# Inducing-point attention with a PReLU feed-forward layer on one core: the x of batch 1 loaded earlier, in fewer transfers, and its DMA transposes moved forward

## The chip, the cores and the metric

The kernel runs on one core of a Trainium2 chip. The metric is the device time of one execution in microseconds (us). The core has five engines with queues of their own: PE (TensorE, matrix multiply), DVE (VectorE), ACT (ScalarE), POOL (GpSimd) and SP (SyncE, which here does nothing but issue DMAs). DMAs are issued from POOL and from SP and are carried by the core's 16 DMA engines. An engine works through its own instructions in order.

## The reference, cut to what matters

```python
B, N, m, C = (4, 12480, 32, 128)          # x: [B, N, C], inducing: [m, C]
def mab(q, kv):
    s = scale * (q @ kv.transpose(0, 2, 1))
    a = softmax(s)                         # written out with max and sum in the reference
    return a @ kv
h   = mab(I, x)                            # 32 inducing points look at all 12480 tokens of a batch
y   = mab(x, h)                            # every token looks at the 32 rows of h
# the second part, over all B*N = 49920 tokens; w_in [128, 2048], w_out [2048, 128]
t = y @ w_in
g = np.maximum(t, 0.0) + alpha * np.minimum(t, 0.0)
out = g @ w_out
```

So a batch has two passes over its x: the first makes `h` (32 x 128) out of all its tokens, and only then can any of its output be made.

## The kernel before, in words

A batch's 12480 tokens are cut into six blocks of 2048 tokens (u = 0 to 5) and a remainder of 192 (u = 6), taken in `order = [0, 1, 6, 2, 3, 4, 5]`. The output side works on groups g of 512 tokens, four to a block, 25 to a batch.

*First pass.* For batch 0 it is the prologue: x is loaded and turned by PE (`p_xpose`, `p_scores`, `p_pool`). For the batches 1 to 3 it runs beside the output work of the batch before, block by block, in four steps:
- `a_load` (L162): DMAs on POOL bring a block of x into a tile `xn`, cast to bf16, cut into `pieces` DMAs. The pool of `xn` has 6 buffers.
- `a_xpose` (L180): one DMA transpose on SP turns `xn` into `xT`. That pool has 8 buffers (XTS).
- `a_scores` (L310): PE multiplies `xT` by the inducing points, ACT takes exp into `e1`, and SP issues a second DMA transpose, `e1T<-e1` (L321; `e1Tr<-e1r`, L331, for the remainder).
- `a_accum` (L336): PE multiplies `e1T` by `xn` and DVE adds to `hacc`.

When all seven blocks are in, `h_sum`, `h_den`, `h_transpose` and `h_weights` make the batch's `hW`.

*Output side.* `b_scores` (L416) makes the scores of a block against h, writes them to DRAM (`e2d<-e`, L435), `b_rep` (L440) reads them back four times as `rep` (L445), `b_den` and `b_turn` send the denominators the same way (`rt<-rd` L478, `rdT<-rt` L488; all four on SP). For each group 16 chunks are made by `fill`: a PE product `hW` x `rep` into a PSUM bank, which ACT (L542) or DVE (L545) empties as relu into a tile `gt`. PE multiplies `gt` by `W1`, and `finish` (L581) closes the group: DVE turns it (L592), POOL multiplies by the reciprocals (L595) and issues four output DMAs (L608).

*Order of the work.* The order on every engine is written out by hand: `pin` chains each engine's instructions. After the prologue come eight sessions t = 0 to 7, in which groups 0 and 1 of batch 0 are filled by four row strips at once, then a step SESSIONS = 8, then the laned stage, in which the groups pass one after another through four lanes of 32 rows; T0 = 9 is the step at the start of its first group, T0 + m the one at the start of its group m. A table `tasks` gives each step the extra work done there, in the order in which `at` entered it. For batch 1 it is set by the lists `score`, `load` and `cross`: the step at which a block, in the order above, is scored, loaded and turned. A block is accumulated 4 steps after it is scored (the last block 3).

*The prologue's end.* POOL's order there is: x of batch 0, `w_in_b` (L635), `w_out_f` in four DMAs (L640), small constants, then `w_scale` (L682) twice: four products for `W1` (W on the page) and four for `AW` (L686). SP's order is: `winT` (two transposes, L693), `e2d` of block 0, and on. PE uses `W1` from the first session on, `AW` and `winT` at t = 5 (`w_amat`).

Of the kernel before, what the change touches and what calls it, by code (L numbers as in the profile page):

```python
# [19 lines left out]
NQ = 4  # L20
# [16 lines left out]
def kernel(  # L37
# [26 lines left out]


    last = {}

    def pin(bi):
        ins = bi.ins
        e = ins.engine  # L70
        if e in last:
            tc.add_manual_dep(
                ins,
                last[e],
                mybir.DependencyInfo(
                    mybir.DependencyClass.NoSync, mybir.DependencyReason.DATA
                ),
                reason="program order",
            )
        last[e] = ins.name  # L80
        return bi
# [30 lines left out]
    def bank():  # L112
        i = min(idle, key=lambda i: clk.free[i])
        idle.remove(i)
        clk.pe = max(clk.pe, clk.free[i])
        return banks[i]

    def drained(t, engine, ns, pe=0, after=190):
        clk.pe += pe
        start = clk.pe + after  # L120
        if engine == "A":
            clk.act = end = max(clk.act, start) + ns
        else:
            clk.dve = end = max(clk.dve, start) + ns
        i = number[id(t)]
        clk.free[i] = end + 170
        idle.append(i)
# [8 lines left out]
    def new_batch(b):  # L136
        st = Batch()
        st.b = b
        st.xT = {}
        st.xTr = xt_pool.tile([C, JR, PR], bf16, name="xTr", tag="xTr")  # L140
        st.xn = {}
        st.e1T = {}
        st.sc = scale
        st.rs = None
        st.e2 = {}
        st.d = {}
        st.rep = {}
        st.rden = {}
        st.rt = {}
        if b > 0:  # L150
            st.es = work.tile([P, NS + 1], f32, name="es", tag="es")
            st.hacc = work.tile([P, C], f32, name="hacc", tag="hacc")
            nc.vector.memset(st.es[:], 0.0)
            nc.vector.memset(st.hacc[:], 0.0)
        return st
# [6 lines left out]
    def a_load(st, u, pieces=1):  # L162
        t0 = u * SUP
        if u < NS:
            xn = xn_pool.tile([P, NQ, GRP], bf16, name="xn", tag="xn")
            src = x[st.b, t0 : t0 + SUP, :].rearrange("(p q j) c -> p q (j c)", q=NQ, j=NB)
            w = NQ // pieces
            for i in range(pieces):
                pin(nc.gpsimd.dma_start(  # L169
                    out=xn[:, i * w : (i + 1) * w, :], in_=src[:, i * w : (i + 1) * w, :]  # L170
                ))
        else:
            xn = xn_pool.tile([PR, JR, C], bf16, name="xnr", tag="xnr")
            pin(nc.gpsimd.dma_start(
                out=xn[:],
                in_=x[st.b, t0 : t0 + REM, :].rearrange("(p j) c -> p j c", j=JR),
            ))
        st.xn[u] = xn
# [56 lines left out]
    def p_scores(st, u, i):  # L235
        blocks = p_blocks(st, u, i)
        pp, nb = (PR, JR) if u == NS else (P, 2 * NB)
        ps = bank()
        for k, (xt, _) in enumerate(blocks):
            mm(ps[:pp, k * M : (k + 1) * M], xt, IT[:])  # L240
        e1t = head_pool.tile([P, 2 * NB, M], bf16, name="e1t", tag="e1t")
        pin(nc.scalar.activation(  # L242
            out=e1t[:pp, :nb, :].rearrange("p k m -> p (k m)"), in_=ps[:pp, : nb * M],
            func=EXP, scale=scale,
        ))
        drained(ps, "A", 370, 200)
        st.e1T[u, i] = e1t
# [243 lines left out]
    def shape_of(g):  # L491
        return (P, NB, 1) if g < NS * NQ else (PR, JR, 2)

    states = {}
    accs = {}
    left = {}
    begun = set()
# [116 lines left out]
    order = [0, 1, NS] + list(range(2, NS))  # L614
# [16 lines left out]
    pin(nc.sync.dma_start(out=al_f[:], in_=moe_alpha.rearrange("(k p) -> k p", p=P)))  # L631
    for u in order[3:]:
        a_load(st, u, pieces=2)
    w_in_b = const.tile([C, DFF], bf16, name="w_in_b")
    pin(nc.gpsimd.dma_start(out=w_in_b[:], in_=moe_w_in))  # L635
    w_out_f = stage.tile([P, KC, C], f32, name="w_out_f", tag="stage")
# [36 lines left out]
    def alphas():  # L673
        alp = bank()
        pin(nc.tensor.transpose(alp[:, :KC], al_f[:], ident32[:KC, :KC]))
        pin(nc.vector.tensor_copy(out=alT[:], in_=alp[:, :KC]))
        pin(nc.vector.tensor_scalar(
            out=om_al[:], in0=alT[:], scalar1=-1.0, scalar2=1.0, op0=MULT, op1=ADD
        ))
        drained(alp, "D", 300, 60)  # L680

    def w_scale(dst, fac):  # L682
        for j in range(NJ):
            f = fac[:, j::NJ]
            fb = bass.AP(tensor=f.tensor, offset=f.offset, ap=[f.ap[0], f.ap[1], [0, C]])
            pin(nc.gpsimd.tensor_tensor(  # L686
                out=dst[:, j::NJ, :], in0=w_out_f[:, j::NJ, :], in1=fb, op=MULT
            ))
# [27 lines left out]
    n = len(halves)  # L716
    p_xpose(st, *halves[0])
    for i in range(n):
        if i + 1 < n:
            p_xpose(st, *halves[i + 1], last=i + 2 == n)  # L720
        p_scores(st, *halves[i])
        if i == n - 1:
            warm(st)
        if i > 0:
            p_pool(st, *halves[i - 1], first=i == 1)
        if i == 3:
            alphas()
            w_scale(W1, om_al)
            w_scale(AW, alT)
            w_inT()  # L730
# [14 lines left out]
    def tokens(st):  # L745
# [21 lines left out]
        SESSIONS = 8  # L767
        T0 = SESSIONS + 1

        tasks = {}  # L770

        def at(t, fn):
            assert t >= 0, t
            tasks.setdefault(t, []).append(fn)
            if not {"b_rep", "b_turn", "a_load", "a_xpose", "h_sum", "new_batch"} & set(fn.__code__.co_freevars):
                pauses.add(t)
# [9 lines left out]
        for b in range(B):  # L786
            base = T0 + (first[b, 0] if b else -2)
            for s in range(1, NS + 1):
                t = base + 4 * s - AHEAD if b or s > 2 else 4 * s - 2
                nt = t + 4 if s < NS else t + 2  # L790
                at(t, lambda b=b, s=s: b_scores(states[b], s))
                at(t + 1, lambda b=b, s=s: b_rep(states[b], s))
                at(nt, lambda b=b, s=s: b_den(states[b], s))
                at(nt + 1, lambda b=b, s=s: b_turn(states[b], s))
            if b + 1 < B:
                n = b + 1
                E = base + 4 * NS
                if b:
                    lag = (-8, -4, -4, 0, 4, 8, 10) if b > 1 else (-4, 0, 0, 4, 6, 8, 10)
                    score = [base + k for k in lag]  # L800
                    load = [t - 7 for t in score]
                    cross = [t - 5 for t in score]
                    late = 4
                else:
                    score = [T0 + k for k in (2, 4, 4, 6, 8, 10, 11)]
                    load = [0, 0, 5, SESSIONS, T0 + 1, T0 + 3, T0 + 5]
                    cross = [5, 5, 6, T0 + 1, T0 + 3, T0 + 5, T0 + 7]
                    late = 3
                for u, k, c, t in zip(order, score, cross, load):
                    at(k + (late if u == order[-1] else 4), lambda n=n, u=u: a_accum(states[n], u))  # L810
                    at(k, lambda n=n, u=u: a_scores(states[n], u))
                    at(c, lambda n=n, u=u: a_xpose(states[n], u))
                    at(t, lambda n=n, u=u: a_load(states[n], u, pieces=NQ))
                at(score[-1] + 1, lambda n=n: h_sum(states[n]))
                H = score[-1] + late
                at(H, lambda n=n: h_den(states[n]))
                at(H + 1, lambda n=n: h_transpose(states[n]))
                H += 2
                assert H <= E - 6
                at(H, lambda n=n: h_weights(states[n]))  # L820
                at(H, lambda n=n: b_scores(states[n], 0))
                at(H, lambda n=n: h_linear(states[n]))
                at(H + 1, lambda n=n: b_rep(states[n], 0))
                at(E - 4, lambda n=n: b_den(states[n], 0))
                at(E - 3, lambda n=n: b_turn(states[n], 0))
                fn = lambda n=n: states.setdefault(n, new_batch(n))
                tasks.setdefault(load[0], []).insert(0, fn)

        def run_tasks(t):
            for fn in tasks.pop(t, []):  # L830
# [44 lines left out]
        while queue or moving or any(tile):  # L875
            best = []
            taken = {q for _, q, _ in moving}
            for f in range(4):
                if tile[f]:
# [3 lines left out]
                    elif (*y, todo[0]) in seen:  # L883
                        t = max(free_at[f], seen[*y, todo[0]][1] - 100)
                        best.append((t, 1, f, "piece"))
                else:
# [3 lines left out]
                    if f == 0 and queue and sum(map(bool, tile)) + len(moving) < LANES:  # L890
                        ch = (*queue[0], 0)
                        if ch in seen:
                            t = max(free_at[f], seen[ch][1] - 100 - SLOT)
                            best.append((t, 2, f, "start"))
            if fillable():
                since = max(min(clk.free[i] for i in idle) - 40, landed.get(need[0][:2], 0))
                hungry = min(clk.act, clk.dve) < clk.pe + HUNGRY
                for f in range(4):
                    t = max(free_at[f], since)
# [8 lines left out]
            t, _, f, what = min(best, key=lambda x: (max(x[0], clk.pe), x[1]))  # L908
# [27 lines left out]
            else:  # L936
                y, todo = tile[f]
                u = todo.pop(0)
# [67 lines left out]
```

## Time and profile before

| what | value |
|---|---|
| device time, three runs | 573.31, 574.81, 575.17 us; median 574.81 us |
| the profiled execution | 575.11 us; span 573.3 us from first to last instruction |
| mean granted PE clock | 0.980 |
| PE busy | 549.9 us, 96% of the span |
| ACT busy | 509.1 us, 89% |
| DVE busy | 499.5 us, 87% |
| POOL busy | 414.8 us, 72% |
| x loads on POOL (L169) | 72 DMAs of 128 KB, 10 of 256 KB |
| xT DMA transposes on SP | 18; issue 2.0 to 7.3 us, landing 6.2 to 16.1 us after the issue began |
| e1T DMA transposes on SP | 18; issue 1.2 to 2.2 us, landing 3.1 to 9.0 us after the issue began |

Times in the text are us from the start of the span, unless they are durations. In a line of the timeline the first number is the start, the second the duration, "xN" says that N instructions were merged, and brackets tell how long the engine was idle before it. PEclk is the granted clock, 1.00 being full speed. SPq stands for SP's queue of DMA issues. In the traces a batch or a block has no number; which block a DMA carries follows from the order above.

### The profile page before, as it was taken

The page shows a single profiled execution, that of the slowest core. Times are in us where ns is not written, and L with a number is a line of the kernel's source. Part 1 is how long each engine was busy: PE and PEld are TensorE (multiplying, and loading weights), DVE is VectorE, ACT ScalarE, POOL GpSimd, SP SyncE. Part 2 cuts the span into 40 slices and gives each one's busy share as a digit, 9 for nine tenths or more (in the row PEclk, how much of TensorE's full clock was granted, in tenths as well). Part 3 has the DMA queues.
Part 4 walks back from the last instruction along what each step waited for, and adds up shares of the span by engine and source line. Part 5 has one row for each costly group of instructions (what it writes and reads, how often), then busy time and mean ns, then how long its engine had stood idle before and what let it go on. Part 6 is the DMA issues. An engine that isn't in the chain of part 4 may idle for free.

```text
span 573.3 us, 21059 instructions
## 1 busy us (share of the span) xinstructions
PE 549.9 (96%) x8671; PEld 300.6 (52%) x8671; DVE 499.5 (87%) x857; ACT 509.1 (89%) x1014; POOL 414.8 (72%) x612
## 2 busy tenths in 40 slices
PE   4999996999999999999999999999999999999994
PEld 4633552555554545555555555655555555555542
DVE  3687895899989999999998999999988999999971
ACT  2477995999998999999989999999999999999970
POOL 6657584687798499886878976675777677676771
PEclk9995998999999999999999999999999999999998
DMA  9979999996899999987897898544444354444333
GB/s 197 223 140 152 187 139 134 156 166 93 139 168 157 111 166 164 159 140 120 128 177 142 114 163 146 77 91 97 67 88 102 56 100 105 80 75 66 57 56 63
DMA packets 120448, 71.09 MB, mean 124 GB/s; under 512 B 87536, under 2 KB 112480, under 8 KB 120352
## 3 DMA queue, kind: packets, MB, share of 16 engines
q0 software_dynamic: 25008, 38.53, 44.3%
q1 hardware_dynamic: 95200, 30.69, 30.4%
q8 instruction: 68, 1.11, 0.9%
q10 hardware_dynamic: 144, 0.52, 0.2%
q14 instruction: 28, 0.23, 0.2%
HBM read 41.00 MB, written 28.95 MB: 122 GB/s over the span
## 4 chain that ended last, share of the span: by engine, by line
PE 58%; POOL 19%; issue 9%; DMA 6%; ACT 5%; DVE 1%; SPq 1%; POOLq 0%; DVEq 0%; ACTq 0%
PE bank L130 58%; POOL out_dram L608 13%; POOL ob L595 6%; ACT gt L542 5%; DMA xn<-in_x_dram 3%; DMA e1T<-e 2%; DVE gt L545 1%; DMA rdT<-rt 1%; SPq L608 1%; DMA rt<-rd 1%; DMA out_dram<-ob 0%; DVE ot L592 0%; DVE hW L302 0%; PE bank L215 0%; ACT xT L224 0%
## 5 line engine op out<-in xcount | busy, mean ns | idle before, releaser
L130 PE MATMUL bank<-gt,W 32*128 32x512 bf16 (+2 forms) x6016 | 497.4, 377 | 0.6
L542 ACT ACTIVATE gt<-bank 128x512 bf16<-128x512 f32 (+1 forms) x920 | 472.7, 608 | 20.8 <-PE bank L130 17.3
L545 DVE TENSOR_SCALAR gt<-bank 128x512 bf16<-128x512 f32 (+1 forms) x648 | 411.9, 679 | 33.5 <-PE bank L130 28.2
L130 PE MATMUL bank<-rep,hW 32*128 32x512 bf16 (+1 forms) x1600 | 418.5, 374 | 0.8 <-DVE hW L302 0.3
L130 PEld LDWEIGHTS <-W 32*128 32x128 bf16 (+1 forms) x6016 | 232.0, 92 | 171.0 <-issue 89.3
L608 POOL DMA_DIRECT2D out_dram<-ob x384 | 245.9, 667 | 47.9 <-POOL ob L595 28.2
L595 POOL TENSOR_TENSOR ob<-ot,rdT 128x512 f32<-128x512 f32 (+1 forms) x100 | 109.3, 1093 | 92.3 <-DVE ot L592 80.6
L130 PEld LDWEIGHTS <-hW 32*128 32x128 bf16 x1600 | 130.4, 92 | 45.6 <-issue 23.8
L592 DVE STREAM_TRANSPOSE ot<-bank 128x512 f32<-128x512 f32 (+1 forms) x100 | 69.4, 695 | 11.9 <-PE bank L130 11.0
L169 POOL DMA_DIRECT2D xn<-in_x_dram x82 | 46.1, 635 | 4.7 <-DMA xn<-in_x_dram 2.8
L130 PE MATMUL bank<-rep,hA 32*128 32x512 bf16 x94 | 35.7, 384 | 0.9 <-DVE hA L302 0.6
L316 ACT ACTIVATE e<-bank 128x512 bf16<-128x512 f32 x18 | 10.9, 605 | 5.3 <-PE bank L130 5.3
L130 PEld LDWEIGHTS <-hA 32*128 32x128 bf16 x94 | 8.5, 92 | 9.9 <-issue 7.6
L242 ACT ACTIVATE e1t<-bank 128x256 bf16<-128x256 f32 (+1 forms) x13 | 4.8, 372 | 10.0 <-PE bank L130 9.9
L427 ACT ACTIVATE e<-bank 128x512 bf16<-128x512 f32 x18 | 11.0, 611 | 2.9 <-PE bank L130 2.7
L221 DVE COPY xT<-bank 128x1024 bf16<-128x1024 bf16 (+1 forms) x12 | 8.0, 669 | 4.5 <-PE bank L215 4.2
L130 PE MATMUL bank<-xn,e1T 128*32 128x128 bf16 x288 | 7.1, 220 | 4.7 <-DMA e1T<-e 4.7
L130 PE MATMUL bank<-xT,hT 128*32 128x512 bf16 (+1 forms) x98 | 10.6, 398 | 0.0
L349 DVE TENSOR_TENSOR hacc<-bank,hacc 128x128 f32<-128x128 f32 x18 | 5.0, 276 | 5.9 <-issue 4.8
L215 PE MATMUL bank<-ident,xn 128*128 128x128 bf16 x96 | 8.6, 246 | 1.2 <-DVE xn L709 0.9
L130 PEld LDWEIGHTS <-e1T 128*32 128x32 bf16 x288 | 5.6, 96 | 7.5 <-DMA e1T<-e 5.2
L130 PEld LDWEIGHTS <-e 128*128 128x128 bf16 x96 | 4.3, 97 | 7.8 <-issue 7.7
(89 smaller groups left out, 132.4 us busy)
## 6 DMA issues: line engine op xcount, KB each, us to landing
out_dram<-ob POOLq DMA_DIRECT2D x372, 64.0 KB, 3.6
rep<-e2d SPq DMA_DIRECT2D x92, 128.0 KB, 3.6
xn<-in_x_dram POOLq DMA_DIRECT2D x72, 128.0 KB, 6.5
e2d<-e SPq DMA_DIRECT2D x24, 128.0 KB, 3.6
xn<-in_x_dram POOLq DMA_DIRECT2D x10, 256.0 KB, 8.7
rdT<-rt SPq DMA_DIRECT2D x96, 8.0 KB, 2.8
w_out_f<-in_moe_w_out_dram POOLq DMA_DIRECT2D x4, 256.0 KB, 10.8
out_dram<-ob SPq DMA_DIRECT2D x12, 64.0 KB, 2.2
```

Of the source, the lines that this page charges most:

```text
L130: return pin(nc.tensor.matmul(o, lhsT, rhs, start=start, stop=stop, **kw))
L169: pin(nc.gpsimd.dma_start(out=xn[:, i * w : (i + 1) * w, :], in_=src[:, i * w : (i + 1) * w, :]))
L215: pin(nc.tensor.transpose(tp[:, k * P : (k + 1) * P], xn[:, q, j * C : (j + 1) * C], ident[:]))
L221: pin(nc.vector.tensor_copy(out=dst, in_=tp[:, :w]))
L316: pin(nc.scalar.activation(out=e1[:], in_=ps[:], func=EXP, scale=scale, accum_out=st.es[:, u : u + 1]))
L349: pin(nc.vector.tensor_tensor(out=st.hacc[:], in0=ps[:, :C], in1=st.hacc[:], op=ADD))
L427: pin(nc.scalar.activation(out=e2[:].rearrange("p (t j i) -> p t j i", j=n, i=32), in_=turned(ps[:pp, :w], n), func=EXP, scale=scale_of(st ...
L542: pin(nc.scalar.activation(out=gt[:, :w], in_=ps[:, :w], func=RELU))
L545: pin(nc.vector.tensor_relu(gt[:, :w], ps[:, :w]))
L592: pin(nc.vector.transpose(out=ot[:, :t], in_=acc[:, :t]))
L595: pin(nc.gpsimd.tensor_tensor(out=ob[:, :t].rearrange("p (k m c) -> p k m c", k=nb, c=32), in0=ot[:, :t].rearrange("p (k m c) -> p k m c", ...
L608: pin((nc.sync if ending else nc.gpsimd).dma_start(out=dst[a], in_=ob[32 * a : 32 * a + 32, :t].rearrange("p (b k) -> p b k", k=32),))
```

## The change

The batch state of batch 1 is made in the prologue, and its blocks u = 0 and 1 are loaded there, on POOL ahead of `w_scale`. The other loads and the transposes of batch 1 move to earlier steps, and each block of batch 1 is loaded in two DMAs instead of four. Scores and accumulations stay at their steps, and so do the batches 2 and 3.

| block u | load before | load after | transpose before | transpose after | score | accumulate |
|---|---|---|---|---|---|---|
| 0 | 0 | prologue | 5 | 5 | T0+2 | T0+6 |
| 1 | 0 | prologue | 5 | 5 | T0+4 | T0+8 |
| 6 | 5 | 0 | 6 | 6 | T0+4 | T0+8 |
| 2 | 8 | 0 | T0+1 | 7 | T0+6 | T0+10 |
| 3 | T0+1 | 3 | T0+3 | T0 | T0+8 | T0+12 |
| 4 | T0+3 | 6 | T0+5 | T0+2 | T0+10 | T0+14 |
| 5 | T0+5 | 8 | T0+7 | T0+5 | T0+11 | T0+14 |

```diff
@@ prologue @@
         if i == 3:
             alphas()
+            states[1] = new_batch(1)
+            for u in order[:2]:
+                a_load(states[1], u, pieces=2)
             w_scale(W1, om_al)
             w_scale(AW, alT)
             w_inT()
@@ tokens @@
                     score = [T0 + k for k in (2, 4, 4, 6, 8, 10, 11)]
-                    load = [0, 0, 5, SESSIONS, T0 + 1, T0 + 3, T0 + 5]
-                    cross = [5, 5, 6, T0 + 1, T0 + 3, T0 + 5, T0 + 7]
+                    load = [None, None, 0, 0, 3, 6, SESSIONS]
+                    cross = [5, 5, 6, 7, T0, T0 + 2, T0 + 5]
                     late = 3
                 for u, k, c, t in zip(order, score, cross, load):
                     at(k + (late if u == order[-1] else 4), lambda n=n, u=u: a_accum(states[n], u))
                     at(k, lambda n=n, u=u: a_scores(states[n], u))
                     at(c, lambda n=n, u=u: a_xpose(states[n], u))
-                    at(t, lambda n=n, u=u: a_load(states[n], u, pieces=NQ))
+                    if t is not None:
+                        at(t, lambda n=n, u=u, k=NQ if b else 2: a_load(states[n], u, pieces=k))
...
                 fn = lambda n=n: states.setdefault(n, new_batch(n))
-                tasks.setdefault(load[0], []).insert(0, fn)
+                if b:
+                    tasks.setdefault(load[0], []).insert(0, fn)
```

(`states = {}` moves to the top of the function.)

More of the change, by code (lines that the diff above doesn't have):

```diff
@@ L66 @@
     last = {}
+    states = {}
     def pin(bi):
@@ L492, in shape_of @@
         return (P, NB, 1) if g < NS * NQ else (PR, JR, 2)
-    states = {}
     accs = {}
@@ L633 @@
         a_load(st, u, pieces=2)
+    nx = []
     w_in_b = const.tile([C, DFF], bf16, name="w_in_b")
```

## The prediction, as it was put on record

> **What bounds the kernel now.** I read the chain of waits in order of time first, and looked on it for stretches that belong to batch 1's first pass. From 100 us on, PE, ACT and DVE are all close to full up to the tail (last row of the third fence), so a stretch saved early moves all that follows forward; a stretch that only adds work to POOL or SP costs nothing until PE waits for it. One link stands out (start, duration, what):
>
> ```profile
> 76.28 3.93 PE bank L130 x71
> ...
> 83.86 9.02 DMA e1T<-e
> 92.92 3.78 PE bank L130 x40
> ```
>
> A DMA transpose of exp scores, issued at 83.86, is waited for by PE. The waits in the window 60 to 100 give the price:
>
> ```profile
> PE bank L130 <- DMA e1T<-e: 4.7, 1, 4.7
> ```
>
> It is step T0+8: block 1's `a_accum` is next on PE, and PE is in order, so the fills behind it stop too and ACT and DVE run dry. The busy time in four stretches shows that, and a second loss behind it (columns: stretch, length, busy PE, PEld, DVE, ACT, POOL, granted clock, DMA share, GB/s):
>
> ```profile
> 60.00:88.00 28.00, 27.84 (x466) 15.43 (x460) 26.20 (x45) 27.30 (x57) 19.34 (x28) 1.00 1.14 165
> 88.30:92.90 4.60, 0.00 (x0) 0.00 (x0) 0.33 (x1) 0.57 (x2) 2.53 (x4) 1.00 1.22 137
> 92.90:96.60 3.70, 3.68 (x50) 1.51 (x54) 1.96 (x4) 1.28 (x3) 0.00 (x0) 0.54 1.06 219
> 100.00:130.00 30.00, 29.85 (x528) 16.03 (x527) 27.48 (x52) 28.51 (x58) 22.94 (x33) 1.00 0.97 158
> ```
>
> PE does nothing for 4.7 us, then runs 3.7 us at clock 0.54, which loses 3.7 x 0.46 = 1.7 us more. Together 6.4 us. As a check, ACT, which is busy 97.5% of 60 to 88, is busy 1.85 us of the 8.3 us from 88.3 to 96.6 instead of 8.1: 6.2 us lost. So 6.4 us is the most that clearing this wait can bring.
>
> Why was the transpose late? Its scores were multiplied at 66.8 (PE, `xT` x `IT`), 17 us before it was issued. SP's timeline says what stood ahead of it:
>
> ```profile
> 43.00 5.85 SPq L183 DMA_TRANSPOSE xT<-xn  x2
> ...
> 59.93 0.34 SPq L478 DMA_DIRECT2D rt<-rd  x1
> 60.46 6.81 SPq L183 DMA_TRANSPOSE xT<-xn  x1
> 67.37 2.35 SPq L488 DMA_DIRECT2D rdT<-rt  x4
> 69.81 0.38 SPq L435 DMA_DIRECT2D e2d<-e  x1
> 70.29 2.16 SPq L321 DMA_TRANSPOSE e1T<-e  x1
> 74.52 1.80 SPq L445 DMA_DIRECT2D rep<-e2d  x4
> 76.50 7.27 SPq L183 DMA_TRANSPOSE xT<-xn  x1
> 83.86 1.53 SPq L321 DMA_TRANSPOSE e1T<-e  x1
> ...
> 92.50 0.50 SPq L478 DMA_DIRECT2D rt<-rd  x1
> ```
>
> SP is 10 to 17 us behind PE. Issuing one xT transpose holds it up to 7.27 us while x loads share the DMA engines, and 4.10 and 3.82 us later (101.31 and 122.71). POOL's timeline shows which loads:
>
> ```profile
> 23.67 4.22 POOL L686 TENSOR_TENSOR W<-w_out_f,om_al 128x512 bf16<-128x512 f32 x4 [3.44 <-DVE rs L285]
> 31.86 4.32 POOL L169 DMA_DIRECT2D xn<-in_x_dram  x8
> 49.48 2.31 POOL L169 DMA_DIRECT2D xn<-in_x_dram  x4
> 59.38 2.11 POOL L169 DMA_DIRECT2D xn<-in_x_dram  x4 [0.25 <-PE bank L130]
> 74.92 2.29 POOL L169 DMA_DIRECT2D xn<-in_x_dram  x4
> ```
>
> Blocks 2, 3 and 4 load between 49.5 and 70, beside the 6.81 us transpose; block 5 from 74.9, beside the 7.27 us one.
>
> **The change part by part.** *Front loads.* Four DMA issues on POOL ahead of `w_scale`. POOL ends its constants at 20.24 and starts the first product at 23.67, with 3.44 us idle; four issues of some 0.55 us (row: 530 to 724 ns, median 573, in the prologue) need 2.3. A POOL or SP issue also waits until the one eight before it has landed: SP's rep at 59.19 is issued 0.02 us after xTr, eight issues back, landed (51.21 + 7.96), and the prologue's loads on POOL show the same spacing. By it the fourth front load waits for `w_in_b` (landed 22.63), goes at 22.9 and ends at 23.5. Cost nothing, hidden in that idle; if the cover were gone, the last W1 product, now done at 27.89 and used by PE about 28.4, would be up to 2.3 - 0.5 = 1.8 us late. The state's two memsets have no input, 0.23 us of DVE, and ran at 1.0 before: nothing.
>
> *Their transfers.* They queue behind `w_out_f` (landed 26.49) and fill 26 to 33, where DMA was free. Beside them run `winT`, `e2d` and block 0's `rep`. Bounds for such a transfer: `rep` landed in 1.8 to 2.7 us without loads (29.85) and in 6.7 to 7.3 with them (35.94; there twice the bytes). At worst block 0's `rep` lands at 38.5 instead of 33.3; its first fill is PE's at 39.56. Nothing on the path, but SP's chain rep, rt, e2d, rep, rdT can come up to 2 us later.
>
> *Other loads.* POOL issues 6, 2, 3, 4 right behind `AW` at 31.9 (7 issues instead of 9), all landed around 45 to 47: halves came 1.25 us apart in the prologue (2.5 us a block), quarters 0.7 to 1.9 us apart at 31.86 (about 3.6 a block). All `xn` buffers are free of batch 0 by 23, so none waits. Block 5 goes at 49.5. From 56 to 92 no x load is in flight. Twelve issues fewer for the whole batch (six blocks, two each) save POOL 12 x 0.55 = 6.6 us, which nobody waits for.
>
> *SP's queue.* The transposes of blocks 0 and 1 keep their place: the first is released at 43.0 by the landing of the `rep` eight issues back (35.94 + 6.98 = 42.92), not by its x (landed 39.3). But block 3's is now ahead of `e1T` of block 0, and block 4's ahead of `e1T` of block 1: one more in each case. So worked out: 43.0; two transposes 5.85, rt, e2d, xTr as before, rt landed, rdT and rep done at 59.5 as before; transposes of blocks 2 and 3 at 4.1 each (rows 3.82 to 7.27; I take 101.31, which also had outputs and no loads beside it): 67.7. Then rt, which hid its landing behind a transpose before (59.93) and no longer does: 4.3 (row 92.50), 72.0; rdT and e2d 2.35 + 0.38 and gaps: 75.0. `e1T` of block 0 goes at 75.0 instead of 70.29 and lands 4.4 us on (its own row), 79.4. PE's first use of it was at 77.7: **a new wait of 1.7 us at T0+6**, behind which stand that step's fills. Its clock costs between nothing (the 0.64 us stop before 39.34 left it at 1.00 up to 45.4) and 1.7 x 1.7 / 4.7 = 0.6; I take nothing, the stop being nearer to the short one. Then e1T 2.2, block 4's transpose 4.1, rep 1.8: `e1T` of block 1 at 83.3, `e1Tr` at 84.9, landing about 5 later (rows 4.4, and 5.5 behind a transpose), 88.4 and 90.0; PE, moved by 1.7, asks at 88.3 + 1.7 = 90.0. I put 0.2 there. After that SP has no xT until block 5's, due long before its scores at T0+11.
>
> *The sum.* -6.4 + 1.7 + 0.2 = -4.5. The profiled execution has 575.11 (span 573.3 and 1.8 around it), 0.3 above the median of the three runs: 570.6, which I call **570.5**.
>
> **Two rules weighed.** The trace shows `rep` three times slower beside loads. The Trainium skill, "DMA: Bandwidth & Descriptors", section "Issuing engines are not separate DMA queues", says that DMAs of all issuers end on the same 16 engines and interleave; by it the front loads take from SP's transfers, against this change, and if SP's chain starts 2 us later for it the result is 572.5. The trace shows the clock at 0.54 behind the 4.7 us stop. "TensorE: Matmul & The Clock Gate" of the Trainium skill, Part 1, has it halve after an idle window of about 3.4 us; by that the new 1.7 us wait costs no clock, where the traced proportion (1.7 for 4.7) would add 0.6.
>
> **The rivals.** *Wait gone altogether:* the transposes go at 3.1 us (spacing of the landings of blocks 0 and 1: 49.24 and 52.29) and SP starts earlier; `e1T` of block 0 is 2 us or more sooner than reckoned. 575.1 - 6.4 = 568.7. For it: no load beside them. Against: rt's landing is exposed. *Wait only moved:* SP 2.6 to 5.1 us later than in my sum, PE waits 4.5 to 7 us in all: 568.7 + 4.5 = 573.2 to 568.7 + 7 = 575.7, about no change. For it: any slip on SP's chain from 26 us on adds to it. *Slower:* the transposes stay as slow as they were, because outputs and not loads hold them. At 6.81 + 7.27 instead of 8.2, `e1T` of block 0 goes at 81 and, landing in 4.4 to 9.0 us (the two rows), PE waits 7.7 to 12 us; block 1's follows at 81 + 2.2 + 5.3 + 1.8 = 90.3 and adds little; clock 1.7. Net +3 to +7: about 580. It decides from a pair of issues above some 13 us on. For it: at 87.05, with no new load issued since 77, one still took 5.33. *Not as described:* the front loads hold `w_scale` (above, 1.8 us), and gain 2.7: 572.4.
>
> **How the numbers follow.** About 0.3% (1.7 us) is what a measurement of this kernel can tell from no change. Chances: forecast, with a remaining wait of 0.6 to 4 us, 0.43, and the held `w_scale` 0.05; wait gone 0.22; only moved 0.14; slower 0.16. The "moved" case lies mostly within 0.3%. Likeliest case alone: 568.7 + 0.6 to 568.7 + 4, 569.3 to 572.7. The range, 567.5 to 576, takes in the gone and the moved case and about 1 us of run spread, and leaves the slower one out. Another stretch at half clock, 45.4 to 59.1, lies where the lanes start; PE's program there is the same, so I let it stand, and 1.7 us more or less of it would stay within the range.
>
> **What would show it.** Right: no x load on POOL between 56 and 92; xT issues after 56 near 4 us; PE's wait for `e1T` at T0+8 gone, one below 2.5 us at T0+6; clock 1.00 around 93; `w_scale` still at 23.7. Wrong: xT issues of 6 to 7 us without loads, rt landing over 6 us, a wait of PE before 40 us for `W1` or `rep`, or a second stretch at half clock.

## The result, and the profile after

The changed kernel is slower: 577.72 us (median of 14 runs, 576.14 to 581.31) against 574.64 us (median of the 14 runs shown beside them, 569.90 to 577.99); ratio 1.006, 95% interval 1.0038 to 1.0083. Here and below the ratios leave out executions more than 1.5% above the fastest of their kernel, while the medians are of all. The profiled execution has 576.56 us, its span is 574.7 us, 1.4 more than before.

The wait that was to go did go. Of the lines shown of before, `PE bank <- DMA e1T<-e` has no counterpart after; SP's timeline of after has at the places shown above:

```profile
22.56 5.24 SPq L694 DMA_TRANSPOSE winT<-w_in_b  x2
27.84 1.58 SPq L436 DMA_DIRECT2D e2d<-e  x1
34.10 2.06 SPq L446 DMA_DIRECT2D rep<-e2d  x4
...
49.19 6.65 SPq L184 DMA_TRANSPOSE xT<-xn  x2
...
66.93 6.05 SPq L184 DMA_TRANSPOSE xT<-xn  x2
...
77.52 2.06 SPq L322 DMA_TRANSPOSE e1T<-e  x1
...
86.43 2.08 SPq L322 DMA_TRANSPOSE e1T<-e  x1
```

The transposes of blocks 2 and 3 hold SP for 6.05 us together (6.81 and 7.27 before). But the first three lines are the trouble. Before, they were

```profile
22.64 3.49 SPq L693 DMA_TRANSPOSE winT<-w_in_b  x2
26.18 0.58 SPq L435 DMA_DIRECT2D e2d<-e  x1
29.85 1.73 SPq L445 DMA_DIRECT2D rep<-e2d  x4
```

`winT`, `e2d` and block 0's `rep` go one behind the other on SP, and each now runs beside x loads. `winT` landed 9.6 to 10.2 us after its issue (4.1 to 4.7 before), `e2d` 6.25 us after (3.7), `rep` 6.3 to 7.5 us after (1.8 to 2.7). The chain of waits of after holds the last two links (start, duration until the landing):

```profile
27.84 6.25 DMA e2d<-e
...
35.69 7.45 DMA rep<-e2d
```

So `rep` is all there at 43.1 instead of 33.3. PE's timeline of after shows it arriving, one row strip at a time (in brackets PE's idle time before the instruction, and what ended it):

```profile
40.48 0.38 PE L131 MATMUL bank<-rep,hW 32*128 32x512 bf16 x1 [0.93 <-DMA rep<-e2d]
41.37 0.38 PE L131 MATMUL bank<-rep,hW 32*128 32x512 bf16 x1 [0.50 <-DMA rep<-e2d]
42.30 0.37 PE L131 MATMUL bank<-rep,hW 32*128 32x512 bf16 x1 [0.55 <-DMA rep<-e2d]
43.19 0.60 PE L131 MATMUL bank<-rep,hW 32*128 32x512 bf16 x1 [0.51 <-DMA rep<-e2d]
```

The last of the four takes 0.60 us instead of 0.38: the clock has halved. The busy time in three stretches of after (columns as above) tells for how long:

```profile
39.40:43.20 3.80, 1.31 (x6) 0.20 (x4) 0.69 (x1) 1.09 (x2) 0.00 (x0) 0.97 1.15 225
43.00:66.90 23.90, 22.91 (x141) 7.51 (x144) 14.25 (x22) 13.53 (x26) 8.56 (x12) 0.50 0.82 143
66.90:100.00 33.10, 32.94 (x562) 18.50 (x555) 30.75 (x52) 31.98 (x67) 18.45 (x26) 1.00 0.90 156
```

Before, the half clock ran from 45.4 to 59.1 (13.7 us):

```profile
42.00:45.40 3.40, 3.16 (x23) 1.25 (x22) 3.40 (x6) 3.26 (x7) 0.00 (x0) 1.00 0.83 162
45.40:59.10 13.70, 13.59 (x99) 4.23 (x99) 8.86 (x15) 9.29 (x18) 11.74 (x18) 0.50 1.10 156
```

After, it ran from 43.0 to 66.9 (23.9 us), with ACT and DVE busy 57% and 60% of it. The account of the two profiled executions: waits for `rep` 0.93 + 0.50 + 0.55 + 0.51 = 2.5; half clock 10.2 us longer, at half rate 5.1; together 7.6 lost. The wait at T0+8 and the half clock behind it, 4.7 + 1.7 = 6.4, gained. Net +1.2; measured +1.4. The medians differ by more, 3.1: the kernel before was profiled at a mean clock of 0.980, and 29 runs of it beside the first experiments have 0.973 to 0.992, median 0.983, while all 14 runs of the changed kernel have 0.972 to 0.978, median 0.974. (0.983 - 0.974) x 575 = 5.2 us of clock, + 2.5 of waits, - 4.7 of the old wait: +3.0.

### The profile page after: what moved, and what is told of

It is laid out like the page before. It is cut to its first block, busy times and chain, and to the rows that moved or that the text cites. A ratio compares the mean times of both kernels' runs of the same rounds, so it can differ in the third digit from the quotient of the medians.

```text
span 574.7 us, 21041 instructions
## 1 busy us (share of the span) xinstructions
PE 553.3 (96%) x8671; PEld 302.2 (53%) x8671; DVE 500.1 (87%) x857; ACT 509.6 (89%) x1014; POOL 408.0 (71%) x600
## 3 DMA queue, kind: packets, MB, share of 16 engines
q0 software_dynamic: 23280, 38.53, 43.1%
## 4 chain that ended last, share of the span: by engine, by line
PE 81%; DMA 5%; ACT 5%; POOL 3%; issue 2%; DVE 1%; SPq 1%; POOLq 0%; DVEq 0%; ACTq 0%
PE bank L131 80%; ACT gt L542 5%; POOL out_dram L608 2%; PE bank L216 1%; DMA rep<-e2d 1%; POOL ob L595 1%; DMA e2d<-e 1%; DMA ind_f<-in_inducing_dram 1%; DMA out_dram<-ob 1%; DMA rt<-rd 1%; DMA rdT<-rt 0%; SPq L608 0%; DVE gt L545 0%; DVE hW L303 0%; SPq L446 0%
## 5 line engine op out<-in xcount | busy, mean ns | idle before, releaser
L595 POOL TENSOR_TENSOR ob<-ot,rdT 128x512 f32<-128x512 f32 (+1 forms) x100 | 108.9, 1089 | 108.5 <-DVE ot L592 90.6
L170 POOL DMA_DIRECT2D xn<-in_x_dram x70 | 39.5, 634 | 5.5 <-DMA xn<-in_x_dram 2.6
L131 PEld LDWEIGHTS <-hT 128*32 128x32 bf16 (+1 forms) x122 | 5.0, 93 | 6.0 <-issue 4.4
L131 PE MATMUL bank<-xT,IT 128*32 128x512 bf16 x72 | 7.5, 399 | 0.0
L216 PEld LDWEIGHTS <-xn 128*128 128x128 bf16 x96 | 6.8, 112 | 1.1 <-DVE xn L710 1.0
```

What stands on the lines that cost most here:

```text
L131: return pin(nc.tensor.matmul(o, lhsT, rhs, start=start, stop=stop, **kw))
L170: pin(nc.gpsimd.dma_start(out=xn[:, i * w : (i + 1) * w, :], in_=src[:, i * w : (i + 1) * w, :]))
L216: pin(nc.tensor.transpose(tp[:, k * P : (k + 1) * P], xn[:, q, j * C : (j + 1) * C], ident[:]))
L595: pin(nc.gpsimd.tensor_tensor(out=ob[:, :t].rearrange("p (k m c) -> p k m c", k=nb, c=32), in0=ot[:, :t].rearrange("p (k m c) -> p k m c", ...
```

## The experiments

Each ratio is to runs of the kernel before on the same chip. The first theory, A, was the account above: the front loads slow `winT`, `e2d`, `rep`, and that is the loss. Rival B blamed the other loads moved to 32 us, rival C the chance of the clock.

**Without the front loads.**

```diff
             states[1] = new_batch(1)
-            for u in order[:2]:
-                a_load(states[1], u, pieces=2)
...
-                    load = [None, None, 0, 0, 3, 6, SESSIONS]
+                    load = [0, 0, 0, 0, 3, 6, SESSIONS]
```

> The changed kernel without the front loads: blocks 0 and 1 are loaded at step 0, behind the weights' scaling, still in two DMAs each; all else as changed. Theory A (the front loads slow the chain winT, e2d, rep of block 0 on SP, so PE waits for rep from 39.5 to 43.2 us and the half clock lasts 23.9 instead of 13.7 us): rep of block 0 lands before 35 us as in the kernel before, no wait of PE for it, half clock about 13.7 us, and the wait for e1T at T0+8 mostly gone; 569 to 573 us. Rival B (it is the loads of blocks 2 to 4, moved to 32 us, that slow rep): rep late and the long half clock stay, 576 to 578 us. Rival C (the length of the half clock is chance): time within 1 us of the changed kernel on the mean, half clock anything between 13 and 24 us.

577.2 us, ratio 1.0068 (1.0027 to 1.0109). `rep` landed by 36.3 and nothing waited for it, the half clock near 46 was 6.8 us long, in two stretches of 3.4, with a wait of 1.2 us for the `rep` of block 1 between them: so far A. But the time missed A's range, because a new wait stands at T0+6. The waits of this kernel, window 60 to 100, and its busy time around that place:

```profile
PE bank L131 <- DMA e1T<-e: 5.3, 1, 5.3
```
```profile
76.00:81.30 5.30, 0.01 (x4) 0.01 (x4) 0.36 (x2) 0.70 (x2) 1.64 (x3) 0.89 0.85 137
81.30:87.00 5.70, 5.70 (x68) 2.17 (x72) 2.37 (x4) 2.59 (x6) 0.00 (x0) 0.50 0.83 178
```

`e1T` of block 0 was issued at 77.6 and landed at 81.2; PE asked at 76.0. With the 5.7 us at half clock behind it that costs 5.3 + 2.9 = 8.2 us, more than the 6.4 of the old wait. This is the wait that the prediction had sized at 1.7.

**The front loads alone.**

```diff
             alphas()
+            states[1] = new_batch(1)
+            for u in order[:2]:
+                a_load(states[1], u, pieces=2)
...
-                    load = [0, 0, 5, SESSIONS, T0 + 1, T0 + 3, T0 + 5]
+                    load = [None, None, 5, SESSIONS, T0 + 1, T0 + 3, T0 + 5]
```

> The kernel before with nothing of the change but the front loads of blocks 0 and 1 (two DMAs each, ahead of the weights' scaling); the other loads, their four pieces and all transposes as before. Theory A: rep of block 0 lands at 37 us or later, PE waits for it or the half clock grows, and the wait for e1T at T0+8 shrinks only as far as PE is later; 576 to 582 us. Rival B: e2d and rep as in the kernel before, since no load is in flight after 33 us; 573 to 575 us. Rival C: no wait for rep, half clock by chance.

574.5 us, ratio 0.9982 (0.9943 to 1.0021): no difference, though not for B's reason. `e2d` landed 7.6 us after its issue and `rep` by 39.3, 6 us later than before, with the other loads at their old places: so the front loads alone do that. But 39.3 is just in time for PE. In the profiled execution the clock did not halve near 45 at all, and PE, early, then waited 10.0 us (73.1 to 83.1) for `e1T` at T0+6. What was won early was waited for later. Reading the two together: front loads move `rep` from 33.3 to 39.3, the other loads, issued behind them from 31.9 on, from there to 43.1, and it takes both to make PE wait.

**`winT` later on SP.**

```diff
             w_scale(AW, alT)
-            w_inT()
...
     b_rep(st, 0, 2)
+    w_inT()
...
-        at(5, w_amat)
+        at(7, w_amat)
```

> The changed kernel with the two transposes winT issued on SP behind block 0's rep instead of ahead of e2d, and w_amat at step 7 instead of 5. The front loads stay. Theory A: e2d of block 0 is issued near 26 us and rep lands by 38 us, PE does not wait for it, the half clock goes back to about 13.7 us, and the gain at T0+8 shows: 568 to 572 us (up to 1 us more if PE waits for winT at step 7). Rival B: rep still lands after 40 us, behind the loads of blocks 2 to 4: 575 to 578 us. Rival C: rep on time, time as the changed kernel.

585.81 us, ratio 1.0159 (1.0098 to 1.0220); it missed every range. `rep` did land by 38.0, but `winT`, issued at 33.9 beside the loads, held SP for 10.65 us and landed 14 us on, and PE waited 11.1 us for it at `w_amat`. It says nothing for or against A, except that transposes beside loads cost more than I allowed.

**One block in front.**

```diff
-            for u in order[:2]:
+            for u in order[:1]:
...
+                    load = [None, 0, 0, 0, 3, 6, SESSIONS]
```

> The changed kernel with block 0 alone loaded in front; block 1 at step 0. Half the bytes beside winT and e2d. Theory A: e2d of block 0 lands 2 to 3 us earlier than in the changed kernel and rep between 36 and 40 us; if under 39.5 the long half clock is gone and the time is 569 to 573 us, if over it 574 to 577 us. Rival B: as the changed kernel, 576 to 578 us.

576.40 us, ratio 1.0031 (1.0002 to 1.0059). `e2d` landed 1.1 us earlier than in the changed kernel, where A had 2 to 3, and `rep` by 40.3, without a wait of PE; the half clock near 47 was 3.4 us, and at T0+6 PE waited 7.4 us. The landing came between the two others, as a dose would. The time lies in A's range for a late `rep`, but not for its reason, as the long half clock is gone.

So A was half of it. New theory, A2: two chains bind in turn, PE's start through `rep`, and SP's queue through `e1T` of block 0. Four more kernels take away one, the other, and both. "By PE" means that block 0's groups 2 and 3 are made as 0 and 1 are, without the `rep` DMA:

```diff
-    b_rep(st, 0, 2)
...
-        at(1, lambda: b_scores_pe(st, 1))
+        for q in (1, 2, 3):
+            at(q, lambda q=q: b_scores_pe(st, q))
```

and "e1T first" alters SP's order:

```diff
                     at(k, lambda n=n, u=u: a_scores(states[n], u))
+                    if not b and u == order[0]:
+                        tasks[k].insert(0, tasks[k].pop())
...
-                    cross = [5, 5, 6, 7, T0, T0 + 2, T0 + 5]
+                    cross = [5, 5, 6, 7, T0 + 2, T0 + 4, T0 + 6]
```

**The change, with `rep` by PE.**

> The changed kernel, but the scores of block 0's third and fourth group are made on PE and ACT in sessions 2 and 3, as the first two are, so that no rep DMA of block 0 is waited for. Two DMA chains are thought to bind in turn: in the changed kernel PE is held by rep of block 0 (2.5 us of waits, then a half clock of 23.9 us), and is so late at T0+6 that e1T of block 0 is there in time. Theory A2 (two chains in turn): the waits for rep go, the half clock shortens to 3 to 14 us, and a wait for e1T of block 0 of 4 to 9 us with a half clock behind it appears at T0+6, as in the kernel without front loads: 574 to 577 us. Rival D (rep alone was the loss): no wait at T0+6, 569 to 572 us. Rival C (chance clock): half clock as long as in the changed kernel.

570.98 us, ratio 0.9923 (0.9898 to 0.9948), about 1.4% less than the changed kernel. The waits for `rep` are gone, 43.0 to 66.9 runs at full clock, and the wait for `e1T` of block 0 appears, 4.9 us at 72.0, with 3.4 us at half clock behind it:

```profile
43.00:66.90 23.90, 23.89 (x341) 11.60 (x339) 22.98 (x39) 23.67 (x52) 14.12 (x20) 1.00 1.14 184
```
```profile
PE bank L131 <- DMA e1T<-e: 4.9, 1, 4.9
```

That is A2's mechanism; its time was too high because I allowed 3 to 14 us of half clock near 45 and this profile shows none. The profiled execution was the fastest of the six (568.80 us, clock 0.992); the others have 0.984 to 0.990, so some half clock may stand there in them. D's time came true without its mechanism.

**No front loads, e1T first.**

> The kernel without front loads (blocks 0 and 1 at step 0), with SP's order altered: e1T of block 0 first at T0+2, ahead of rdT and e2d, and the xT transposes of blocks 3, 4 and 5 at T0+2, T0+4 and T0+6, behind the e1T of their step, instead of T0, T0+2 and T0+5. Theory A2 (the place in SP's queue makes e1T late): e1T of block 0 is issued before 72 us and lands before PE asks; waits at T0+6 and T0+8 under 1 us, no half clock after 60 us: 567 to 571 us. Rival E (the DMA engines are full whatever the order): e1T lands near 80 us again, 575 to 578 us.

573.27 us, ratio 0.9946 (0.9917 to 0.9974). `e1T` of block 0 was issued at 69.4 and landed at 74.4; no wait for an `e1T` is left, so the order on SP, not full DMA engines, had made it late. Some 2 us slower than expected. The half clock near 46 was as long as before (13.7 us); that is 6.8 us, most of the 7.4 us between this profiled execution (571.57 us) and that of the fastest kernel below (564.21), which has no half clock there.

**The change, e1T first.**

> The changed kernel with the same altered order on SP and nothing else. Theory A2: PE is late there for another reason (rep of block 0), so an earlier e1T brings nothing: 576.5 to 578.5 us. Rival F (SP's order alone is the loss of the changed kernel): 569 to 573 us.

579.34 us, ratio 1.0055 (1.0030 to 1.0079), the changed kernel's own ratio being 1.006: nothing gained, as A2 has it and F has not. PE waits for `rep` and runs at half clock from 43.8 to 67.7.

**The change, both.**

> The changed kernel with both: block 0's third and fourth group by PE and ACT, and the altered order on SP. Theory A2: both chains are out of the way, no wait of PE over 1 us between 39 and 100 us: 566 to 570 us. Rival E: a wait at T0+6 stays, 574 to 577 us.

566.42 us, ratio 0.9828 (0.9805 to 0.9851), faster than both kernels. SP's timeline of it, and its busy time in the stretches of above:

```profile
63.29 1.04 SPq L479 DMA_DIRECT2D rt<-rd  x1
64.43 2.06 SPq L322 DMA_TRANSPOSE e1T<-e  x1
67.90 1.74 SPq L489 DMA_DIRECT2D rdT<-rt  x4
...
75.47 1.24 SPq L322 DMA_TRANSPOSE e1T<-e  x1
```
```profile
39.40:43.20 3.80, 3.16 (x24) 0.96 (x24) 3.27 (x8) 2.40 (x5) 0.00 (x0) 1.00 1.11 230
43.00:66.90 23.90, 23.89 (x338) 11.68 (x339) 22.99 (x39) 23.67 (x51) 13.78 (x19) 1.00 1.10 183
66.90:100.00 33.10, 33.01 (x574) 18.80 (x574) 31.43 (x54) 32.02 (x66) 22.52 (x32) 1.00 0.97 159
```

`e1T` goes in the time that SP used to spend waiting for rt to land, 13 us earlier than in the changed kernel and 10 us earlier than with `rep` by PE alone (74.5). No stop for `rep` or `e1T`, no half clock before the tail, ACT at 99% where it was at 57%. This execution was the fastest of the five (clock 0.996); the other four have 0.989 or 0.990, so some 3.5 us of clock are lost in them, where no profile shows.

**What each part is worth in that company.** First the kernel before with `rep` by PE alone:

> The kernel before with block 0's third and fourth group made on PE and ACT, and nothing of the change. Its rep of block 0 was not waited for. Theory A2: no gain beyond the chance of the half clock at 45 us; the wait for e1T at T0+8 stays at 4 to 9 us: 572 to 576 us. Rival G (the extra PE work in the sessions is what gains, by keeping the clock up, whatever SP does): 567 to 571 us.

575.71 us, ratio 0.9996 (0.9958 to 1.0033): nothing, against G. The profiled execution is the longest of the twelve (580.05 us), so no time is taken from it; it shows PE waiting for `e1T` at T0+6 and T0+8.

The kernel before with both repairs (block 2's transpose at T0+1, as its x is loaded at 8) and its own late loads:

> The kernel before with both repairs of the fastest kernel so far (block 0's groups by PE; on SP e1T of block 0 first at T0+2, xT of blocks 3, 4, 5 at T0+2, T0+4, T0+6), but its own late loads in four pieces. Theory A2 with the loads mattering: xT transposes of blocks 2 and 3 are issued beside x loads, take 6 to 7 us each, and PE waits 3 to 8 us at T0+6 or T0+8 for an e1T or an xT: 570 to 575 us. Rival H (order on SP is all, the earlier loads bring nothing): 565 to 568 us.

572.60 us, ratio 0.9981 (0.9950 to 1.0011). The transpose of block 2, issued at 60.4 beside loads, landed 17.0 us on, `e1T` behind it 12.5 us on, and PE stood 4.2 us around T0+6, 1.5 of them for that `e1T`; for the other 2.7 the profile names no cause. With the same repairs the change's loads make it 566.4: by the ratios (0.9828 and 0.9981, on two chips) the change is worth about 1.5% where its two wait chains are cut.

Both repairs and the change without its front loads:

> The fastest kernel so far without the front loads: blocks 0 and 1 at step 0. Theory A2: with block 0's rep off SP the front loads harm nothing, and they clear the DMA engines 5 us earlier; without them rep of block 1 and the first xT come a few us later, PE waits 0 to 3 us for rep of block 1 near 50 or e1T at T0+6: 567 to 570 us. Rival I (front loads are only harm): 564 to 566 us.

571.24 us, ratio 0.9952 (0.9921 to 0.9983). The first xT, issued at 38.8 with seven or more loads in flight, landed 15.5 us on; PE waited 3.3 us for it at T0+2 and 1.7 us for `e1T` at T0+8. So the front loads are not only harm: without `rep` in their way they are worth about 1.2% (ratios 0.9828 and 0.9952). The time came out above my range, the waits near its upper end.

Both repairs and the change, in quarters:

> The fastest kernel so far with each block of batch 1 loaded in four DMAs instead of two. Theory: the halves matter in the front alone, where the eighth and later issues wait for landings: with quarters w_scale starts 2 to 4 us later and PE waits for W1 near 28 us; 568 to 572 us. Rival: no difference, 565 to 568 us.

570.86 us, ratio 0.9960 (0.9935 to 0.9984). POOL and PE of this kernel:

```profile
26.27 0.53 POOL L170 DMA_DIRECT2D xn<-in_x_dram  x1 [0.29 <-DMA w_out_f<-in_moe_w_out_dram]
...
27.71 4.07 POOL L687 TENSOR_TENSOR W<-w_out_f,om_al 128x512 bf16<-128x512 f32 x4
```
```profile
28.81 0.39 PE L131 MATMUL bank<-gt,W 128*128 128x512 bf16 x1 [0.62 <-POOL W L687]
```

The last front issues wait for the landing of the issue eight before, `w_scale` starts at 27.7 instead of 24.4, and PE waits for four parts of `W1`, 2.3 us in all. Behind these stops the clock is at half from 30.9 to 37.7, which costs up to another 3.4. The halves matter, as expected and there; by the ratios the quarters cost 1.3%, some 7.5 us, of which this is up to 5.7.

## Why the prediction was wrong

It called 570.5 us and a gain of 0.8%; the kernel lost 0.6%.

*The old wait and its price.* T0+8 was cleared, the clock there is 1.00, 6.4 us came back in the profile, so the price was right. That it was cleared in the changed kernel is in part luck: `e1T` of block 1 landed at 90.6, where I had 88.4, and PE had asked for it at 88.3 before. It was there in time because PE came 7.5 us late.

*Front loads on POOL.* Right: the fourth went at 22.83, `w_scale` began at 23.60, its last W1 product ended at 27.9 as before.

*Their transfers: the step that failed.* I took `rep` as the one transfer to be slowed and bounded it by the rows 1.8 to 2.7 and 6.7 to 7.3, which gave 38.5 at worst against PE's 39.56, and "nothing on the path". For `rep` itself that bound nearly held (7.45). But the chain has three links in series on SP, and I left the two ahead of `rep` at their old times. `e2d` was issued 1.7 us later behind `winT` and landed 2.6 us slower; the four `rep` were issued 0.3 us more slowly and landed 4.2 to 5.4 us slower. That is 9.9 in all for the last, and the margin was 6.3. Nor was the stretch from 26 to 33 free: the DMA share there was 0.47 before and is 1.20 after. The first two links are the front loads' doing. The third is that of the other loads, which started at 31.9: with the front loads alone `rep` took its old 1.7 to 2.4 us. I had even written that SP's chain could come 2 us late, and did not add that to the `rep` that PE waits for, though a wait of PE for `rep` before 40 us was among my signs of being wrong. The rule of the Trainium skill ("DMA: Bandwidth & Descriptors", section "Issuing engines are not separate DMA queues") that all issuers share the 16 engines was the right one to weigh: every one of these landings agrees with it, and by it I should have applied the loaded row to all three links.

*Other loads.* Blocks 6, 2, 3 and 4 had landed by 45.3, as reckoned. Block 5's went at 54.6, not 49.5, and was in flight until 63.0, beside the second xT transpose, which landed 10.2 us after its issue.

*The half clock near 45.* I let it stand because PE's program was the same. It grew by 10.2 us: 5.1 us, twice the waits that went with it. That is the larger half of the loss. In the two kernels whose profile shows PE waiting for `rep` in that stretch (the change, and the change with e1T first) it lasted 23.9 us both times, and in all their 25 runs the mean clock is 0.969 to 0.978, median 0.974, against medians of 0.982 to 0.984 of the kernel before on the three chips. In the profiles of the kernels that make `rep` by DMA and do not wait for it, the half clock there lasted 13.7, 6.8, 0, 3.4 and 13.7 us (leaving out `winT` later on SP, which has the stop of 11.1 us there); in those that make it by PE, 0 or 3.4. That the wait lengthens it is shown; how long it is without one stays open.

*SP's queue and the new wait at T0+6.* The mechanism was right, its size was not. In the changed kernel the wait does not appear, since PE is 7.5 us late by then (85.2 instead of 77.7) and `e1T` (issued at 77.5, where I had 75.0) is there. Without the front loads it is 5.3 us plus 2.9 of clock, where I had 1.7 and nothing: SP's start came 2.8 us later, at 45.8, PE, with less half clock, asked 1.7 us earlier, and the clock did halve. Pricing that clock in proportion to the wait was wrong as well, since it goes in steps (last section). The transposes themselves were together no slower than my 8.2 us: 2.7 and 3.3 in the changed kernel, 3.5 and 4.4 without the front loads.

*The rivals.* "Slower" had its chance, 0.16, but another mechanism: in the changed kernel the two transposes held SP for 2.7 and 3.3 us and not for 6.8 and 7.3. No output was issued beside them, so that outputs would not hold them is not shown. "Wait only moved", 0.14, is what the kernel without front loads shows.

## What to carry to other kernels

When a load is moved into a free stretch of the DMA engines, price every transfer that runs there, and where they depend on one another add the delays up before comparing with the margin of the first reader. A wait that goes may only uncover the next chain: against the kernel before, cutting either of the two chains of the changed kernel brought at most 0.8%, cutting both 1.7%. In a queue that runs in order, put the short transfer that somebody waits for ahead of the one that must first wait itself.

## What the runs showed of the hardware

- The time from issue to landing of the same xT transpose (512 KB) ran from 4.3 us to 18.5 us in these kernels, the longest beside x loads, and the issue itself held SP for 1.7 to 7.3 us in the kernels before and after.
- In all 14 traces no DMA issue on POOL or SP starts before the landing, where the trace has it, of the issue eight before on the same queue. Among the front loads it shows as gaps of 0.3 to 1.4 us between issues, on SP at 43.0 in the kernel before as one of 2.0. Whether the chip or the program's own semaphores set that limit, no run here tells.
- The granted clock changed in steps. In each of the 14 traces all its changes but the one at the very end lie on a grid of 3.41 us, and before the tail a half clock lasted 3.4, 6.8, 10.2, 13.7 or 23.9 us. So a stop costs either no clock or at least one step, 1.7 us of work where PE is the bound, and not a share by its length.
- The clock halved without one long stop: in the changed kernel PE had four stops of 0.5 to 0.93 us, with six matmuls between 39.4 and 43.2, and it then stayed at half for 23.9 us although PE was busy for 22.9 of them. In the kernel before it halved at 45.4 although PE was busy for 3.16 of the 3.4 us ahead of it. The rule of "TensorE: Matmul & The Clock Gate" in the Trainium skill, Part 1, an idle window of about 3.4 us to halve and a busy one to restore, agrees with the 4.7 us stop at T0+8 and not with this. What differs is the number of matmuls and not PE's busy time: 141 in those 23.9 us, 338 in the same stretch of the fastest kernel, which kept the full clock with the same kind of 32-row work. That too few matmuls let the clock fall and hold it down is read from this; no run varied it alone.
